# Leaving out some of the dummy matmuls among the last products and column sums of the first q

## The chip, the cores and the metric

The kernel runs on one core of a Trainium2 chip. The metric is the device time of one execution in microseconds (us). The profile counts from the start of the core's span, which is about 1.8 us shorter than the device time (809.5 and 811.27 us in the profiled execution of the kernel before).

PE is the matmul engine and PEld its weight load, which overlaps with PE (790.1 and 385.5 us busy in a span of 809.5 us). DVE and ACT are the vector and the scalar engine. POOL here issues the loads from memory, and SP issues transposes by DMA and stores.

## The reference, cut to what matters

```python
# q, k, v: (4, 6016, 256)
qn = q / (norm(q, axis=1) + 1e-6);  kn = k / (norm(k, axis=1) + 1e-6)
a  = softmax(kn.transpose(0, 2, 1) @ qn / tau)     # (4, 256, 256)
x  = (v @ a).reshape(24064, 256)
out = (silu(x @ w_gate) * (x @ w_val)) @ w_out     # d_ff = 1536
```

The kernel never makes x. For each batch it multiplies the 256 x 256 softmax into w_gate and w_val, in "units" of 128 x 512, and then runs v through the products (Wg and Wv). So the first batch has a start-up part that nothing hides: load k and q, form k-q products and norms, take the softmax, form the units. Then comes the dense stage, in which PE is busy to the end. The start-up of the other three batches runs in the background of the batch before.

## The kernel before: what the change and the argument touch

`keep_warm` is a matmul of ones that nobody reads. The loop over groups forms, for the last groups of q, the products and then the sums of squares column by column.

```python
    def keep_warm(n):
        ps = psum_o.tile([P, 2, C], FP32, tag="o")
        for _ in range(n):
            nc.tensor.matmul(ps, ones_bf, warm_bf, start=True, stop=True)
    # ... cut ...
    load_first_v()
    load_w(0, HW)                  # first half blocks of w_gate and w_val
    load_w(HW, WP)                 # second halves
    load_v(*allc[1])               # second chunk of v, then transposed by DMA
    transpose_v(*allc[1])
    for wc in range(1, NWC):
        load_w(wc * WP, (wc + 1) * WP)       # second and third blocks
    nc.gpsimd.dma_start(out=w_out_sb, ...)
    for g, which, gl in order:     # k groups, then q groups; NQ = 9, G_COLS = 5
        # ... cut: squares on ACT and DVE ...
        if which == 0:
            for t in ts:
                gemm1_pair(0, t)
            if g == G_COLS:
                first_cols(0)
            if g in (NQ - 4, NQ - 3):
                keep_warm(1)
        for t, sq in zip(ts, sqs):
            if which == 0 and g >= G_COLS:
                first_col_sums(0, t, sq)
            # ... cut ...
        if which == 0:
            # ... cut ...
            if G_COLS <= g < NQ - 2:
                keep_warm(NQ - 2 - g)
    first_softmax(0)               # holds three more dummies
```

The dense stage needs the second block of w_gate in its second step (f = 1), since each step forms two units ahead:

```python
        for f in range(FH):
            g_ps, v_ps, mv = gv_matmuls(b, ci, f)
            us = range(2 * f + 2, min(2 * f + 4, len(wp_units))) if gi == 0 else ()
            # ... cut: units us, silu, product, matmul with w_out of the chunk before ...
```

Each unit reads exT, the exponentials of the softmax, as weights. The other batches' norms come to DVE through memory: `norm_cols` writes a row out and reads it back broadcast to all partitions (ink), and `logits` multiplies with it on DVE fourteen steps later.

## Time and profile before

| | kernel before |
|---|---|
| device time, median of the first 3 runs | 812.73 us (812.66 to 813.35) |
| span of the profiled execution | 809.5 us |
| PE busy in the span | 790.1 us |
| PE busy from 40 us to 809 us | 762.4 us |
| last q load seen by DVE, softmax begins on ACT | 33.73 us, 35.04 us |
| second block of w_gate: landed, used by PE | 40.07 us, 40.20 us |

How to read it: from 40 us on PE has hardly a gap, so the last rows tell how early that part starts, and nothing before it counts unless it moves that start. Landing times are those of the loads' signals in the trace. The profile prints times to 0.01 us. The device time scatters (by 0.69 us in these three runs).

### The profile page before, as it was taken

What the parts mean: (1) busy time and instruction counts of PE and PEld (TensorE: products, weight loads), DVE (VectorE), ACT (ScalarE), POOL (GpSimd) and SP (SyncE); (2) the same over time, 40 slices, a digit from 0 to 9 for tenths busy, and PEclk for the clock granted to TensorE, in tenths of its full rate; (3) what the DMA queues carried; (4) which work ended last, traced back from release to release, by engine and by line L of the source; (5) the groups of instructions that cost most, each with busy time, mean ns of one, the idle gap of its engine ahead of it and who ended that gap; (6) DMA issues with size and microseconds to landing.
All of it is one profiled execution on the core that took longest, in us unless ns stands there. A gap on an engine that the chain in (4) does not pass through costs nothing.

```text
span 809.5 us, 11903 instructions
## 1 busy us (share of the span) xinstructions
PE 790.1 (98%) x3905; PEld 385.5 (48%) x3979; DVE 550.1 (68%) x841; ACT 455.6 (56%) x803; POOL 260.9 (32%) x320
## 2 busy tenths in 40 slices
PE   4999999999999999999999999999999999999998
PEld 2644444444454444444454444444445444444446
DVE  4777887658666778766766787866766665665654
ACT  4566666555555666555555666655555555555553
POOL 4415888431011787722010377742100000000000
PEclk9999999999999999999999999999999999999999
DMA  9995999659798899566889799763866656565533
GB/s 90 144 153 106 146 181 170 127 92 163 126 171 141 173 156 159 151 131 73 162 153 146 157 164 181 128 138 80 185 131 143 137 130 131 144 130 129 117 113 98
DMA packets 201070, 112.34 MB, mean 139 GB/s; under 512 B 149088, under 2 KB 187744, under 8 KB 200256
## 3 DMA queue, kind: packets, MB, share of 16 engines
q1 hardware_dynamic: 182720, 84.11, 44.0%
q0 software_dynamic: 18144, 27.41, 31.6%
q8 instruction: 31, 0.51, 0.3%
q14 instruction: 31, 0.25, 0.1%
q10 hardware_dynamic: 144, 0.07, 0.0%
HBM read 79.04 MB, written 60.43 MB: 172 GB/s over the span
## 4 chain that ended last, share of the span: by engine, by line
PE 95%; DMA 3%; issue 1%; ACT 0%; DVE 0%; POOL 0%; ACTq 0%; POOLq 0%
PE g_ps L439 30%; PE v_ps L439 30%; PE o_new L480 29%; PE ps L408 2%; DMA q_sb<-in_q_dram 2%; PE kq_new L168 2%; PE o_new L533 1%; DMA k_sb<-in_k_dram 1%; ACT silu L445 0%; PE last_ps L557 0%; DVE sv L449 0%; PE ss_new L195 0%; PE kq_new L173 0%; PE ps L398 0%; PE unit_ps L408 0%
## 5 line engine op out<-in xcount | busy, mean ns | idle before, releaser
L449 DVE TENSOR_TENSOR sv<-silu,v_ps 128x512 bf16<-128x512 bf16 (+1 forms) x576 | 387.3, 673 | 224.7 <-ACT silu L445 223.5
L445 ACT ACTIVATE silu<-g_ps 128x512 bf16<-128x512 f32 (+1 forms) x576 | 339.1, 589 | 292.9 <-PE g_ps L439 245.1
L439 PE MATMUL v_ps<-vT,Wv 128*128 128x512 bf16 (+1 forms) x1109 | 326.3, 374 | 1.2
L439 PE MATMUL g_ps<-vT,Wg 128*128 128x512 bf16 (+1 forms) x1105 | 325.8, 375 | 1.3
L480 PE MATMUL o_new<-sv,w_out_sb 128*128 128x512 bf16 (+1 forms) x1078 | 318.9, 375 | 1.2
L439 PEld LDWEIGHTS <-Wv 128*128 128x128 bf16 x1152 | 112.7, 98 | 131.0 <-issue 0.6
L300 POOL TENSOR_TENSOR acc_new<-acc_new,sq 128x512 f32<-128x512 f32 x135 | 156.1, 1156 | 56.0 <-DVE sq L290 41.9
L480 PEld LDWEIGHTS <-w_out_sb 128*128 128x128 bf16 x1104 | 108.0, 98 | 126.3
L439 PEld LDWEIGHTS <-Wg 128*128 128x128 bf16 x1152 | 109.6, 98 | 122.2
L126 POOL DMA_DIRECT2D vb_new<-in_v_dram x47 | 24.2, 516 | 265.5 <-DMA vT<-vb_new 264.6
L490 DVE COPY pl<-o_new 128x512 uint16<-128x512 uint16 (+1 forms) x92 | 62.3, 677 | 9.5 <-ACT pl L489 9.5
L290 DVE TENSOR_TENSOR sq<-q_sb 128x512 bf16<-128x512 fp8e5 x72 | 66.5, 924 | 0.0
L489 ACT COPY pl<-o_new 128x512 uint16<-128x512 uint16 (+1 forms) x92 | 53.2, 578 | 19.3 <-PE o_new L480 17.2
L291 ACT ACTIVATE sq<-k_sb 128x512 bf16<-128x512 fp8e5 x72 | 44.2, 615 | 0.0
L168 PE MATMUL kq_new<-k_sb,q_sb 128*128 128x512 fp8e5 x184 | 35.6, 319 | 0.9 <-DMA q_sb<-in_q_dram 0.9
L111 POOL DMA_DIRECT2D q_sb<-in_q_dram x45 | 25.2, 561 | 14.4 <-DMA k_sb<-in_k_dram 9.9
L168 PEld LDWEIGHTS <-q_sb 128*128 128x256 fp8e5 x184 | 22.9, 140 | 9.4 <-DMA q_sb<-in_q_dram 2.0
L195 PE MATMUL ss_new<-sq,ones_bf 128*128 128x256 bf16 x83 | 14.7, 334 | 11.1 <-ACT sq L185 11.1
L111 POOL DMA_DIRECT2D k_sb<-in_k_dram x42 | 22.9, 549 | 1.2 <-POOLq L741 0.8
L295 POOL TENSOR_TENSOR acc_new<-sq 128x512 f32<-128x512 bf16 x3 | 3.5, 1153 | 49.2 <-DVE sq L290 49.2
L195 PEld LDWEIGHTS <-ones_bf 128*128 128x128 bf16 x83 | 9.3, 117 | 15.1 <-issue 10.9
L408 PEld LDWEIGHTS <-exT 128*128 128x128 bf16 x104 | 10.0, 98 | 10.9 <-DMA w_gate_sb<-in_moe_w_gate_dram 0.2
(98 smaller groups left out, 209.0 us busy)
## 6 DMA issues: line engine op xcount, KB each, us to landing
rows<-pl SPq DMA_DIRECT2D x86, 256.0 KB, 3.1
out_dram<-ot_new SPq DMA_DIRECT2D x43, 512.0 KB, 4.0
vb_new<-in_v_dram POOLq DMA_DIRECT2D x43, 256.0 KB, 4.5
q_sb<-in_q_dram POOLq DMA_DIRECT2D x36, 128.0 KB, 6.4
k_sb<-in_k_dram POOLq DMA_DIRECT2D x33, 128.0 KB, 7.1
ot_new<-rows SPq DMA_TRANSPOSE x92, 3.7
k_sb<-in_k_dram POOLq DMA_DIRECT2D x5, 256.0 KB, 9.0
rows<-pl SPq DMA_DIRECT2D x6, 192.0 KB, 2.4
```

The source lines that it names most:

```text
L111: nc.gpsimd.dma_start(out=dst[:, gs:gs + gm, :], in_=src[b].rearrange("(p s) c -> p s c", s=NS)[:, gs:gs + gm, :])
L168: nc.tensor.matmul(kq[:, jh, :], q_sb[:, ps:ps + 2, js], k_sb[:, ps:ps + 2, :], start=(t == 0 and jh == 0), stop=last, perf_mode=DR, skip_ ...
L290: nc.vector.tensor_mul(sq[:, :pm, 0, :], q_sb[:, ps:ps + pm, :], q_sb[:, ps:ps + pm, :])
L291: nc.scalar.activation(sq[:, :pm, 1, :], k_sb[:, ps:ps + pm, :], ACT.Square)
L300: nc.gpsimd.tensor_tensor(out=acc, in0=acc, in1=sq[:, s, :, :], op=ALU.add)
L408: nc.tensor.matmul(ps, state[b, "exT"][:, jh, ih * P:(ih + 1) * P], (w_gate_sb, w_val_sb)[w][:, jh, cols], start=(jh == 0), stop=(jh == CH ...
L439: nc.tensor.matmul(dst[:, :mv], W[:, kk, fs], vT[:, kk, :mv], start=(kk == 0), stop=(kk == CH - 1))
L445: nc.scalar.activation(silu[:, :mv], g_ps[:, :mv], ACT.Silu)
L449: nc.vector.tensor_mul(sv[:, f, :mv], silu[:, :mv], v_ps[:, :mv])
L480: nc.tensor.matmul(self.o_ps[h][:, :self.mv], w_out_sb[:, f, h * P:(h + 1) * P], self.sv[:, f, :self.mv], start=(f == 0), stop=(f == FH - 1))
L489: nc.scalar.copy(pl[:, 0, :self.mv], halves[:, 0, :self.mv])
L490: nc.vector.tensor_copy(pl[:, 1, :self.mv], halves[:, 1, :self.mv])
```

## The change

The intent is to save PE time where dummies stand in front of real work. By its name, `keep_warm` is there for PE's clock; whether the clock needs these dummies was measured below (granted clock 1.00 from 26.40 to 40.05 us in q_none_sm, which has none).

```diff
-            if g in (NQ - 4, NQ - 3):
+            if g == NQ - 4:
                 keep_warm(1)
@@
-            if G_COLS <= g < NQ - 2:
-                keep_warm(NQ - 2 - g)
+            if g == G_COLS:
+                keep_warm(1)
```

With NQ = 9, group 5 had one dummy ahead of and two behind its sums, and group 6 one ahead and one behind. One ahead and one behind stay, in group 5.

## The prediction

> **What bounds the kernel now.** I read the page first, for which engine sets the span.
>
> ```profile
> span 809.5 us, 11903 instructions
> ...
> PE 790.1 (98%) x3905; PEld 385.5 (48%) x3979; DVE 550.1 (68%) x841; ACT 455.6 (56%) x803; POOL 260.9 (32%) x320
> ```
>
> PE (TensorE) is busy for 790.1 of 809.5 us, and from 40 us to the end the busy table by windows gives it 762.4 of 769.0 us. So there every microsecond by which PE starts that stage earlier, without meeting another wait, comes off the end. The change lies before it, in the last groups of the first q. There I read the chain of waits, in order of time.
>
> ```profile
> 32.88 0.46 PE ps L398 x2
> 33.34 0.44 PE kq_new L168 x4
> 33.77 0.23 PE ps L398
> 34.00 0.18 PE cols L218 x8
> 34.18 0.24 PE ps L398
> 34.42 0.22 PE kq_new L168 x2
> 34.64 0.23 PE kq_new L173 x2
> 34.87 0.14 PE cols L218 x6
> ...
> 35.04 0.18 ACT inq L224
> ```
>
> L398 is the dummy matmul, L168 and L173 the k-q products, L218 the column sums. The reader is to see that the dummies are not idle filling: between 32.88 and 35.01 each stands in PE's order ahead of real products or sums, and the softmax on ACT starts when the last sum is done. Then I asked whether PE would have had anything to do earlier, from the timelines of DVE and of PE with its weight loads.
>
> ```profile
> 33.73 0.42 DVE L182 TENSOR_TENSOR sq<-q_sb 128x256 bf16<-128x256 fp8e5 x1 [0.39 <-DMA q_sb<-in_q_dram]
> ```
> ```profile
> 39.76 0.59 PE L439 MATMUL v_ps<-vT_new,Wv 128*128 128x512 bf16 x2
> 40.20 1.03 PE L408 MATMUL ps<-w_gate_sb,exT 128*128 128x512 bf16 x4
> ```
> ```profile
> 40.11 0.61 PEld L408 LDWEIGHTS <-exT 128*128 128x128 bf16 x4 [0.25 <-DMA w_gate_sb<-in_moe_w_gate_dram]
> ```
>
> The columns are start, length, engine, line, operation; the bracket is the idle time before and what ended it. The square of the last q row waits for its load until 33.73 and ends at 34.15. At 40.11 the weight load for the second block of w_gate waits for a load from memory: it is released just in time for its matmul at 40.20, which follows the one before without a gap.
>
> [...] there is one cold window of 3.41 us, between two warm ones.
>
> ```profile
> 15.85:19.26 3.41, 1.59 (x12) 1.05 (x11) 1.90 (x3) 1.77 (x4) 0.97 (x2) 1.00 1.07 107
> 19.26:22.68 3.42, 3.29 (x15) 2.41 (x14) 1.72 (x4) 2.16 (x6) 0.62 (x2) 0.50 1.07 107
> 22.68:26.09 3.41, 2.98 (x27) 2.38 (x26) 2.21 (x6) 1.39 (x4) 0.53 (x1) 1.00 1.07 107
> 26.09:29.50 3.41, 2.97 (x26) 2.45 (x27) 2.75 (x5) 2.14 (x4) 1.44 (x2) 1.00 1.08 104
> ...
> 32.92:36.33 3.41, 3.41 (x39) 2.37 (x37) 2.08 (x7) 1.67 (x5) 3.09 (x5) 1.00 1.48 222
> ```
>
> After the length of each window come PE, weight loads, DVE, ACT and POOL busy, then the granted clock. A window with PE busy for 1.59 us (47%) was followed by a half clock; windows with 2.97 us (87%) were not. The window of the change has 3.41. [...] the two dummies behind the first sums start 215 ns apart, though each is shown 378 ns long, since the shown lengths overlap.
>
> **The change part by part.** The label speaks of four dummies of six. Comparing the instruction order of the two kernels, I count five in these groups before and two after, so three matmuls and their three weight loads go: the second of the pair behind the first group's sums, the one ahead of the second group's sums, and the one behind them. The other engines' orders are the same, no real matmul moves against another, and two allocations fewer in the two-deep rotation of that PSUM tag leave every later tile on the same buffer.
>
> Removed: 3 x 0.215 us = 0.65 us of PE time; the weight loads (96 ns each) lie beside matmuls and give nothing. All 0.65 us lie on the chain. What bounds them next: the last six sums start at 34.71 now and would start at 34.71 - 0.65 = 34.06; the last two of them read the square that ends at 34.15, plus some 0.05 us for the signal (the gap that the chain shows between engines is 0.02 to 0.05), so 34.20 where they start at 34.81 now. **That gives 0.6 us** at the start of the softmax: its first ACT instruction would move from 35.04 to about 34.4, the first product with exT from 36.66 to about 36.05.
>
> What the later stage meets when it comes 0.6 us early: the landings on the load queue, which PE does not steer. The loads are issued by POOL between 26 and 36 us, each released by an earlier landing, and the load engines are saturated there (share 1.0 to 1.5 in the windows). From the times of the landing signals in the trace, with the time of the first matmul that needs each: first v chunk 34.83 (needed 35.48), first half block of w_gate 35.48 (36.66), of w_val 36.16 (36.87), second half of w_gate 36.88 (37.60), of w_val 37.55 (38.90), **second block of w_gate 40.07 (40.20)**, of w_val 41.33 (42.04), third of w_gate 42.59 (43.77). Those up to 38.90 have at least 0.65 us of slack, so the 0.6 us just passes them. The second block of w_gate has 0.13 us, of which the signal and the weight load (0.04 + 0.10) use all. So PE would be ready at 40.20 - 0.6 = 39.6 and wait until 40.20: -0.65 from the dummies, +0.05 for the square, +0.6 in the new wait. **Sum: about 0.** From 40.20 on PE would be where it was, and the rest of the span is the same program. If the landing moves a little against PE from one execution to the next, some 0.1 us of the 0.6 may survive, so I expect 812.73 - 0.1 = 812.6 us.
>
> **Rivals.** First, the whole 0.6 us survives (812.1 us): that needs the second w_gate block to land 0.6 us earlier in relation to PE in the timed executions. For it: I see one execution only, and that one took 811.27 us where the timed ones took 812.66 to 813.35. Against it: q and w_gate share one saturated queue, so they shift together. Second, the clock falls: [...] PE runs up to 3.4 us at half clock. If that hits the dense stage from 36 us on, it loses at most 1.7 us, of which up to 0.6 us was to be waited for w_gate anyway, so +1.1 to +1.7 us, about 814.1 us. For it: the clock did fall in this kernel at 47% busy[...]. Against it: after the change no PE gap between 31 and 40 us is estimated above 0.6 us, and the window of the change keeps roughly 3.41 - 0.65 = 2.8 us busy or more (81%), since real work moves up into it[...]. [...] this keeps a chance of some 8%. Third, transfers hide everything already before the change, the q loads being the bound: I put 0.05 us of the 0.65 down to that; it would be more if the last q row landed later than 33.7, and the outcome is again zero.
>
> **Range and chances.** The centre is 812.6. Downwards the full 0.65 us plus the spread of the kernel before (0.7 us from lowest to highest) gives 811.6; upwards half a cold window or the same spread gives 813.6. Two per cent would be 16.3 us, 25 times the PE time removed and nearly ten times the worst cold window, so either side gets one per cent.
>
> **What would show it right or wrong.** In the changed profile: (1) L398 on PE three fewer (records of single matmuls can be missing, so count its weight loads: 8 before, 5 after); (2) the first ACT instruction on the column sums some 0.6 us earlier in relation to the last q square; (3) a PE wait of about 0.6 us on the load of w_gate just ahead of the second block's matmuls near 40.2 us, where there was none; (4) granted clock 1.00 from 23 us on; (5) from there the same PE busy time to the end. I would be wrong if the clock shows 0.50 in any window after 30 us, if no wait on w_gate appears and the end is 0.6 us earlier, or if the time moves by over 1.5 us, which nothing here can explain.

0.65 us off for three dummies (215 ns between the starts of two of them), 0.05 us back for the square and 0.6 us back for the new wait come to about 0, and the 0.1 us that may survive gives 812.6 us. A "warm" window is a stretch with the granted clock at 1.00, a "cold" one a stretch with 0.50. The 1.7 us of the second rival are an estimate from the one record of 3.41 us at 0.50: in it matmuls of 256 columns start 213 to 214 ns apart, in the record of 1.00 before it mostly 108 to 109 ns. In q_before_v, run later, two such stretches at 0.50 follow each other. The 8% is the author's estimate; in the one trace there was then, nothing between 47 and 87% busy had been seen at a recorded clock.

## The result, and the profile after

| | before | after |
|---|---|---|
| device time, median of 4 runs | 813.04 us (812.66 to 813.95) | 813.19 us (811.37 to 813.47) |
| ratio after / before | | 0.9995 (0.9978 to 1.0013) |
| span of the profiled execution | 809.5 us | 811.6 us |

The interval in brackets behind a ratio is the 95% one. Ratios are the mean time of one kernel's fast runs over that of the other's of the same rounds, so not quite the ratio of the medians quoted. The lines below answer to those that the prediction shows of before. First PE's timeline of the changed kernel (start, length, engine, line, operation, count, and in brackets the idle time before with what ended it):

```profile
32.61 0.38 PE L398 MATMUL ps<-warm_bf,ones_bf 128*128 128x512 bf16 x1
32.75 0.67 PE L168 MATMUL kq_new<-k_sb,q_sb 128*128 128x512 fp8e5 x4
33.50 0.35 PE L218 MATMUL cols<-ones_bf,sq 128*128 128x1 bf16 x8
...
34.19 0.38 PE L218 MATMUL cols<-ones_bf,sq 128*128 128x1 bf16 x6
...
39.28 0.59 PE L439 MATMUL v_ps<-vT_new,Wv 128*128 128x512 bf16 x2
40.28 1.04 PE L408 MATMUL ps<-w_gate_sb,exT 128*128 128x512 bf16 x4 [0.41 <-DMA w_gate_sb<-in_moe_w_gate_dram]
```

Only one dummy is left behind the first sums, products follow sums directly, and PE is done with its second step about half a microsecond earlier (39.28 instead of 39.76). Then it stands still. The bracket's 0.41 us counts from the modelled end of the matmul before; by starts, the next matmul would have followed at 39.71 (two matmuls, 0.216 us each) and came at 40.28, which is 0.57 us lost. The weight load ahead of it shows the same wait from its own side:

```profile
40.27 0.55 PEld L408 LDWEIGHTS <-exT 128*128 128x128 bf16 x4 [0.90 <-DMA w_gate_sb<-in_moe_w_gate_dram]
```

The chain of waits, asked for the stretch from 31 to 43 us, no longer runs over dummies, sums and softmax. It runs over the load:

```profile
33.65 6.58 DMA w_gate_sb<-in_moe_w_gate_dram
40.23 0.04 issue
40.28 1.04 PE ps L408 x4
```

The softmax itself did start earlier. ACT's first instruction on the column sums, before and then after:

```profile
35.04 0.17 ACT L224 ACTIVATE inq<-cols 128x2 f32<-128x2 f32 x1 [1.10 <-PE cols L218]
```

```profile
34.61 0.17 ACT L224 ACTIVATE inq<-cols 128x2 f32<-128x2 f32 x1 [0.51 <-PE cols L218]
```

In this execution the last q square began at 33.89 instead of 33.73, because its load landed later. Measured from that square, ACT starts 0.72 us after it instead of 1.31 us: 0.59 us earlier.

One step further the two traces differ once more. PE at the second block of w_val, before and then after:

```profile
42.04 1.02 PE L408 MATMUL ps<-w_val_sb,exT 128*128 128x512 bf16 x4
```

```profile
42.02 1.03 PE L408 MATMUL ps<-w_val_sb,exT 128*128 128x512 bf16 x4
```

By the spacing of the starts this matmul comes 0.12 us late in the kernel before (its weight load stands behind 0.24 us of "issue", for which the profile shows no wait) and in time in the changed one. What makes that gap is not shown.

**Where the 2.1 us between the two profiled spans come from.** Step by step the changed kernel is 0.09 us behind at 40.28 us and 0.02 us ahead from 42 us on, and then it falls behind near 184 and near 378 us. The timeline of DVE near 184 us, of before and then of the changed kernel:

```profile
181.71 0.48 DVE L344 SCALAR_TENSOR_TENSOR s_new<-kq_new,inv,ink 128x256 f32<-128x256 f32 x1
```

```profile
183.51 0.48 DVE L344 SCALAR_TENSOR_TENSOR s_new<-kq_new,inv,ink 128x256 f32<-128x256 f32 x1 [1.73 <-DMA ink<-row]
```

DVE waits 1.73 us for the broadcast norms (ink) of the next batch, holds up the products behind it, and PE then waits for DVE (idle for 0.33 us before its matmul at 184.64 us and for 0.90 us before that at 379.69 us). The dummies stand far from this, and the kernel before has timed runs as long (up to 813.95 us), so I take it for a wait that comes in some executions and not in others. So the first experiment made the ground quiet.

### The profile page after: what moved, and what is told of

Same layout as the page of the kernel before. It is cut to its first block, busy times and chain, and to the rows that moved or that the text cites. A ratio compares the mean times of both kernels' runs of the same rounds, so it can differ in the third digit from the quotient of the medians.

```text
span 811.6 us, 11971 instructions
## 1 busy us (share of the span) xinstructions
PE 794.5 (98%) x3976; PEld 385.4 (47%) x3976; DVE 550.2 (68%) x841; ACT 455.3 (56%) x803; POOL 260.6 (32%) x320
## 4 chain that ended last, share of the span: by engine, by line
PE 89%; DMA 9%; POOL 1%; DVE 1%; issue 1%; ACT 0%; DVEq 0%; POOLq 0%
PE g_ps L439 28%; PE v_ps L439 28%; PE o_new L480 27%; DMA row<-inv 3%; PE ps L408 2%; DMA q_sb<-in_q_dram 2%; PE kq_new L168 2%; DMA k_sb<-in_k_dram 2%; DMA ink<-row 1%; PE o_new L533 1%; DMA w_gate_sb<-in_moe_w_gate_dram 1%; DVE sv L449 1%; POOL k_sb L111 0%; POOL inv L330 0%; POOL inv L328 0%
## 5 line engine op out<-in xcount | busy, mean ns | idle before, releaser
L439 PE MATMUL v_ps<-vT,Wv 128*128 128x512 bf16 (+1 forms) x1128 | 330.5, 375 | 1.5 <-DVE sv L449 1.2
L439 PE MATMUL g_ps<-vT,Wg 128*128 128x512 bf16 (+1 forms) x1128 | 330.9, 375 | 0.0
L480 PE MATMUL o_new<-sv,w_out_sb 128*128 128x512 bf16 (+1 forms) x1104 | 324.7, 376 | 0.0
```

The lines of the kernel that those rows point to most:

```text
L439: nc.tensor.matmul(dst[:, :mv], W[:, kk, fs], vT[:, kk, :mv], start=(kk == 0), stop=(kk == CH - 1))
L480: nc.tensor.matmul(self.o_ps[h][:, :self.mv], w_out_sb[:, f, h * P:(h + 1) * P], self.sv[:, f, :self.mv], start=(f == 0), stop=(f == FH - 1))
```

## The experiments

The theory: the three dummies cost PE their full time on the chain, and their removal gives it back, but the second block of w_gate lands when it lands, so PE waits there instead. Rival 1: the dummies only filled time in which PE waited for q anyway. Rival 2: the clock falls without them and eats a gain. Rival 3: there is a plain gain, and the scatter hides it.

**Quiet ground, and the second chunk of v moved: four kernels on one chip.** In all four, `logits` and all that follows it in the background of a batch come three steps later, so that ink has landed:

```diff
-    plan[S1 + 24].append((logits, 0))
+    plan[S1 + 27].append((logits, 0))
     ... and so on with each later step of that plan, + 3
```

The kernels are q_before (the kernel before, so changed), q_after (with the three dummies left out) and the two with a suffix v, in which the load that precedes the suspected one is moved behind it (in this diff and in those below, arguments and repeated lines are put in words):

```diff
     load_w(HW, WP)
+    load_w(WP, 2 * WP, w_gate only)
     load_v(*allc[1])
     transpose_v(*allc[1])
-    for wc in range(1, NWC):
+    load_w(WP, 2 * WP, w_val only)
+    for wc in range(2, NWC):
         load_w(wc * WP, (wc + 1) * WP)
```

> The kernel before, with one thing changed in the other batches only: logits and what follows them come three steps later, so that they find the broadcast of the norms landed. The changed kernel's profile shows about 0.5 and 1.3 us lost there (near 184 and 378 us), the profile of before nothing, and the timed runs lie in two groups near 811.4 and 813.2 us. If that wait is the scatter: about 811.3 us in nearly all runs, ratio to before near 0.998. If not: 813.0 us and the same scatter. It is to be the quiet ground for the three runs beside it.

> The same quiet ground with the three dummies left out. Theory (the time saved goes into a wait for the second block of w_gate): softmax about 0.5 us earlier, PE waits about 0.6 us near 40.2 us for that load, end within 0.1 us of q_before. Rival 1 (the dummies filled time in which PE waited for q anyway): softmax not earlier, no new wait, end the same. Rival 2 (clock): granted clock 0.50 in a window after 30 us, 1 us or more slower. Rival 3 (a plain gain hidden by scatter): 0.6 us faster than q_before.

> q_before with the load of the second v chunk moved behind the second block of w_gate, which should land about 1.2 us earlier. Theory: with the dummies in place PE has no wait there to lose, so within 0.1 us of q_before. Rival (that load held up PE before too): about 0.6 us or more faster.

> q_after with the same move of the v load. Theory: the wait near 40.2 us is gone and the 0.5 to 0.6 us reach the end: 0.5 us faster than q_after, q_before and q_before_v, perhaps 0.05 less because the second block of w_val comes just in time. Rival 1: no difference to q_before_v. Rival 3: no more than q_after already gained.

| 5 timed runs each | median | lowest to highest | mean | PE starts the second w_gate block |
|---|---|---|---|---|
| q_before | 811.01 us | 810.91 to 811.91 | 811.18 | 40.20 us, no wait |
| q_after | 811.40 us | 810.68 to 812.06 | 811.31 | 39.91 us, after a wait |
| q_before_v | 810.98 us | 810.88 to 811.99 | 811.20 | 40.07 us, no wait |
| q_after_v | 810.79 us | 810.40 to 811.10 | 810.75 | 39.64 us, no wait |

The kernel before took 810.99 to 813.50 us in the same rounds. The four never exceed 812.06, and no profile of a kernel with the later logits shows DVE waiting for ink, which fits the ink wait as the upper part of the scatter, though no single ratio to before leaves the noise. One run in five near 811.9 remained; what that is shows below.

The theory's pattern is there. Rival 1 falls: the softmax begins 0.75 us after the last square in q_after (34.19 us) and 1.27 us in q_before (34.98 us). Rival 2 falls in the executions profiled: the granted clock is 1.00 from 24 us on in all four. Rival 3, 0.6 us of plain gain, does not show in the means (811.18 and 811.31 us). PE's timeline of q_after and q_after_v at the second block:

```profile
38.82 0.59 PE L439 MATMUL v_ps<-vT_new,Wv 128*128 128x512 bf16 x2
39.91 1.04 PE L408 MATMUL ps<-w_gate_sb,exT 128*128 128x512 bf16 x4 [0.49 <-DMA w_gate_sb<-in_moe_w_gate_dram]
```

```profile
39.21 0.59 PE L439 MATMUL v_ps<-vT_new,Wv 128*128 128x512 bf16 x2
39.64 1.03 PE L408 MATMUL ps<-w_gate_sb,exT 128*128 128x512 bf16 x4
```

The order of two loads alone makes the wait appear or vanish. With the dummies in place the same move changes nothing in the mean (811.18 and 811.20). Without them it takes 0.56 us off the mean (811.31 to 810.75), where 0.5 was expected. With five runs each the times support this and do not prove it; the positions in the profiles do. In the profiled execution of q_after w_gate landed at 39.86, 0.21 us earlier than in q_before, and its span is the shortest of the four (808.9 us). From 42 us to the end PE is 0.40 us ahead of q_before there, so some 0.19 us of the lead are left even when the earlier landing is taken off.

The profiled execution of q_after_v also shows the next wall. PE at the first use of the moved v chunk:

```profile
52.42 0.61 PE L439 MATMUL g_ps<-vT,Wg 128*128 128x512 bf16 x2 [0.40 <-DMA vT<-vb_new]
```

The chunk's transpose landed at 52.38 (49.28 in before), and there this execution lost again all that it had gained.

**Three dummies more, the load one transfer later, no dummies at all, and a repair: four kernels on a second chip.**

> q_before with three more dummies in the same places (two behind the first group's sums, one behind the second's). Theory: each dummy is 0.216 us on the chain to the softmax and PE reaches the second block of w_gate without slack, so the softmax and everything from there on is 0.65 us later than in q_before and the end too: 811.65 us. Rival 1 (dummies fill time in which PE waits for q): no shift. The same step that is worth nothing downwards should cost its full size upwards.

```diff
-                keep_warm(NQ - 2 - g)
+                keep_warm(4 if g == G_COLS else 2)
```

PE's timeline of q_before, then of q_before_p3:

```profile
32.26 0.39 PE L398 MATMUL ps<-warm_bf,ones_bf 128*128 128x512 bf16 x1
...
34.65 0.29 PE L218 MATMUL cols<-ones_bf,sq 128*128 128x1 bf16 x6
```

```profile
33.47 0.39 PE L398 MATMUL ps<-warm_bf,ones_bf 128*128 128x512 bf16 x1
...
36.52 0.29 PE L218 MATMUL cols<-ones_bf,sq 128*128 128x1 bf16 x6
```

From the first dummy to the last sums q_before_p3 takes 3.05 us; q_before needs 2.39 us. That is 0.66 us more for three dummies, against 0.65 expected, so in this stretch each dummy costs its full 0.22 us. (The 0.216 us of the expectation stand between the starts of the last two dummies in the trace of the kernel before.) The median is 812.27 us; the repeat of q_before on the same chip, told below, has 811.11. That is 1.16 us more where 0.65 was expected. The three fastest runs (811.47, 811.47, 811.75) are 0.4 to 0.7 us above the usual 811.0 to 811.1. The other three took 812.80 to 813.12 us; the one of them that was profiled (813.08 us) had a late q load, for which PE waited 1.17 us. So the positions show the 0.65 us; the timed runs fit it only if the slow three are set aside after the fact.

> q_after with w_val loaded ahead of w_gate in the second block, so that the load under suspicion lands one transfer (1.2 to 1.3 us) later. Theory: the PE wait near 40.2 us grows by 1.2 to 1.3 us and so does the time, to about 812.6 us. Rival 1 and rival 3 (that wait is not what bounds the start of the dense stage): no change.

```diff
-        load_w(WP, 2 * WP)                     # w_gate, then w_val
+        load_w(WP, 2 * WP, w_val, then w_gate)
```

PE's timeline:

```profile
41.26 1.04 PE L408 MATMUL ps<-w_gate_sb,exT 128*128 128x512 bf16 x4 [1.69 <-DMA w_gate_sb<-in_moe_w_gate_dram]
```

The wait grew from 0.49 to 1.69 us, by 1.20 us as expected. The median is 812.36 us. q_after was not on this chip in these rounds, so the pair was run again (below).

> q_after without any dummy at all: the two left in the groups and the three of the softmax are gone too. Theory: no further gain, since the last square of q and then the w_gate load bound PE; the wait near 40 us is about the same or some 0.1 us longer, the time within 0.2 us of q_after, if the clock holds. If the clock falls without dummies (rival 2): granted clock 0.50 in a window between 33 and 40 us, the dense stage 1 us or more later, 812.4 us or more.

```diff
             if g == NQ - 4:
-                keep_warm(1)
...          (all calls of keep_warm, also the two in first_softmax)
```

The busy times of this kernel in stretches of 3.41 us, the length of the clock record at 0.50 in the kernel before (length; PE, weight loads, DVE, ACT, POOL busy; then granted clock, DMA share, GB/s):

```profile
29.81:33.22 3.41, 3.26 (x33) 2.61 (x30) 2.87 (x6) 1.69 (x3) 1.75 (x3) 1.00 1.17 131
33.22:36.64 3.42, 2.81 (x38) 2.11 (x38) 2.43 (x9) 2.02 (x6) 3.08 (x6) 1.00 1.58 243
```

The clock held with PE busy for 2.81 of 3.42 us (82%). PE waits for w_gate by 0.42 us and starts the block at 40.16. The median of 4 runs is 810.95 us (810.61 to 812.12). None of the eight dummies was needed for the clock in this execution, and without the last five the time stayed within the scatter.

> q_after_v, whose gain of 0.4 us was lost again at 52 us because the moved v chunk was transposed late beside the load of w_out: here the second half of w_out is loaded two steps into the dense stage instead. Theory: the transposed chunk lands before 51.8 us, no PE wait at 52 us, and the end is 0.4 to 0.5 us earlier than q_before and 0.3 to 0.5 us earlier than q_after_v, near 810.5 us. If the chunk is late for another reason than w_out, PE waits there as in q_after_v.

```diff
-    nc.gpsimd.dma_start(out=w_out_sb, ...)            # all 256 columns
+    load_w_out(0)                                     # 128 columns
...  (in the dense loop)
+            if now == 2:
+                load_w_out(1)
```

Its profile did what was expected: no wait at 52 us, the moved chunk's matmuls at 51.87 instead of 52.40 in q_before, the span 808.7 us. The timed runs did not follow. They lie between 810.53 and 814.28 us, three of six above 812, median 811.73. Something that the one profile does not show goes wrong in other executions; I did not pursue it, so this stays open. It is no improvement.

**The pair again with its control, and a candidate: four kernels on the second chip.** The first three are the same files as before.

> q_before again, as the control on the chip of the three runs beside it: PE reaches the second block of w_gate near 40.2 us without a wait, about 811.0 us where no load of q straggles.

> q_after again beside its two variants. Theory: within 0.3 us of q_before_2, with a PE wait of 0.4 to 0.6 us on w_gate. A plain gain of the change would show as 0.6 us less.

> w_val ahead of w_gate again, now beside q_after on one chip: by the theory 1.2 to 1.3 us longer than q_after_2 in the same rounds, since the first run showed the wait at 1.69 us where q_after had 0.49; if the wait does not set the end, the same time.

> No dummies at all, and the load of the second v chunk behind the second block of w_gate: the candidate that may beat both kernels. Theory: the clock holds as in q_none_sm, no wait near 40 us, PE about 0.5 us ahead of q_before there; at 52 us PE waits for the transposed v chunk as in q_after_v and loses up to that gain again. So between 810.4 and 811.0 us, at best 0.5 us under q_before_2, and under the kernel before by that and by the norm wait that the later logits avoid.

| runs on the second chip | median | lowest to highest |
|---|---|---|
| kernel before, 12 runs | 812.11 us | 811.23 to 814.51 |
| q_before_2, 6 runs | 811.11 us | 810.92 to 811.91 |
| q_after_2, 4 runs | 811.26 us | 811.02 to 811.52 |
| q_after_vf_2, 4 runs | 812.38 us | 811.95 to 812.40 |
| q_none_sm_v, 6 runs | 810.87 us | 810.50 to 811.40 |

q_after_vf_2 is 1.12 us above q_after_2 by medians and their ranges do not touch. Expected were 1.2 to 1.3; by the profiles PE starts the block at 41.17 instead of 40.25, 0.92 us later. So a shift of that load's landing goes to the end nearly in full. q_before and q_after are equal again: over both chips the mean is 811.25 us for 11 runs with all dummies and 811.29 us for 9 runs without the three.

The control showed something that the prediction had not allowed for. PE in its profiled execution (811.83 us):

```profile
40.97 1.03 PE L408 MATMUL ps<-w_gate_sb,exT 128*128 128x512 bf16 x4
```

PE is 0.77 us late here without any wait for w_gate, which landed at 40.05 as ever. One of the sixteen parts of a q load landed at 32.07, more than a microsecond after the other fifteen (30.71); PE's longest wait for a q load is 1.0 us in this profile and 0.5 us in that of q_before. Two more of the 11 runs of q_before lie near 811.9; they were not profiled, and I take them for the same. The profiled execution of q_after_vf_2 had the same straggler (31.95), and there it cost nothing, since the wait absorbed it:

```profile
39.80 0.59 PE L439 MATMUL v_ps<-vT_new,Wv 128*128 128x512 bf16 x2
41.17 1.04 PE L408 MATMUL ps<-w_gate_sb,exT 128*128 128x512 bf16 x4 [0.78 <-DMA w_gate_sb<-in_moe_w_gate_dram]
```

The wait shrank from 1.69 to 0.78 us, the block began at 41.17 instead of 41.26, and the two executions took 811.95 and 812.03 us. So without the dummies PE has slack in front of the load, and a late q eats into the slack first. The same late load stands in four of the fourteen profiles (also in q_before_p3 and q_none_sm_v), each time 1.2 to 1.5 us behind its other parts.

q_none_sm_v is faster than the kernel before, with a ratio of 0.9983 and an interval of 0.9970 to 0.9995. Most of it comes from the later logits: q_before_2 alone has 0.9986 (0.9973 to 1.0000). It counts as "same" by the 2% bar, and it was not run beside the changed kernel as given. I take it as the best version found. Its profiled execution, the slowest of the six (811.40 us), did not show the expected lead: with a q load late at 32.28 us PE started the block at 40.17, where q_before has 40.20, and it waits 0.19 us for the transposed chunk at 52 us.

## Why the prediction was right, point by point

The measured 813.19 us lies in the range of 811.6 to 813.6 us around 812.6, and "within 2%" was right. A range of 2 us tests little about an effect of 0.6 us, so the steps count more. The lower edge does not follow from its own terms, either: 812.73 less 0.65 and 0.7 is 811.4, and one timed run of the changed kernel took 811.37 us.

1. *Three matmuls go.* Right: the weight loads of the dummy are 8 before and 5 after.
2. *Each dummy stands on the chain with 0.215 us, and the last q square leaves 0.6 us of the 0.65.* Right: 0.59 us earlier measured from that square. Upwards three dummies cost 0.66 us.
3. *The first halves of the weight blocks just let the 0.6 us pass.* Nearly right. The nearest was the first half of w_val, which landed at 36.32 and was used at 36.37, about 0.07 us late by the spacing of the starts.
4. *The second block of w_gate takes it all back.* The mechanism is right: 0.57 us lost by starts where 0.6 was written, in a place where before had no wait. Moving that landing earlier or later moved PE with it. "All" is some 0.2 us too much. The 0.13 us between landing and use were not all needed for the signal and the weight load: in the changed kernel the matmul follows the landing by 0.05 us (40.23 to 40.28).
5. *The clock holds.* Right in every profile taken here, from 24 us on to the last microsecond or so. That PE's busy time from 40 us on stays the same cannot be read off: 762.4 us before and 766.6 us after, but with 3706 and 3776 matmuls on record; the weight loads agree (3776, 365.7 us). The prediction gave the fall 8%, by the author's estimate; with no dummy at all the clock held too (1.00 at 82% busy in q_none_sm).
6. *The q loads and w_gate shift together because they share a queue* (the argument against the first rival). It holds between the first two profiles (the last q load and w_gate each 0.16 us later), but not always: a single late part of one q load moves PE by 0.77 us and leaves w_gate where it was. In such an execution the dummies' removal does save: with the late part at 31.95 us (q_after_vf_2) PE is 0.73 us earlier at the end of its second step than with it at 32.07 us (q_before_2), so by my estimate some 0.6 us are due to the three dummies, and w_gate in its usual place (40.05 us) would have left nearly all of it. How much this gives on average is not shown.
7. *Some 0.1 us may survive.* The times do not resolve it: 813.04 and 813.19 us, and 811.25 and 811.29 us; the difference of the latter two has a 95% interval (my estimate from the single runs) of 0.35 us faster to 0.43 us slower, which leaves out a gain of 0.6 us and not one of 0.2. The profiles do: w_gate landed 0.16 us later in the changed kernel's execution and PE is 0.02 us ahead from 42 us on, and q_after, q_after_2 and q_none_sm against q_before give the same. Reckoned from the landing, 0.18 to 0.19 us survive: 0.08 us of point 4, the rest the gap at 42 us.
8. *A move of over 1.5 us could not be explained.* Single executions do move by 2 us. This was taken for spread without a cause; much of it is the wait of DVE for the broadcast norms in the other batches (1.73 us near 184 us and 2.30 us near 378 us in the changed kernel's profile, none in the profiles with later logits).

## What to carry to other kernels

Before you count a saving on the chain, list the landing times of what the next stage needs beside the times at which it is used. Here a use that followed its landing by 0.13 us had hardly any slack (0.08 us could be used; in the changed kernel the matmul still came 0.05 us after the landing), though the profile showed no idle time of PE at all. Here that co-limit was visible only as 0.25 us of waiting of an engine that overlaps with the bound one (PEld). Taking 0.65 us away ahead of it left some 0.2 us; adding 0.65 us moved the chain by all of it. And where the effect is smaller than the scatter, find what scatters first and judge by positions in the profile.

## What the traces show of the clock and of the parts of a load

- In the kernel before, the trace records a granted clock of 1.00 from 15.85 to 19.26 us, of 0.50 from 19.26 to 22.68 us and of 1.00 from there to the end of the span. In the 3.41 us ahead of the fall PE was 47% busy, and its longest gaps were those in these lines of PE's timeline.

```profile
17.20 1.12 PE L195 MATMUL ss_new<-sq,ones_bf 128*128 128x256 bf16 x8 [0.88 <-ACT sq L185]
19.32 1.65 PE L195 MATMUL ss_new<-sq,ones_bf 128*128 128x256 bf16 x7 [1.00 <-ACT sq L185]
```

- PE's busy time is as the profile shows it, with modelled ends of the matmuls. In eleven of the fourteen profiles the mean granted clock is 0.995 to 0.998, and in the 3.41 us ahead of the first record at 0.50 PE was busy for 1.39 to 1.71 us (41 to 50%). In the other three (q_after, q_best and q_none_sm_v) the mean is 1.0; the lowest stretch read there, in q_after, had 1.81 us (53%), with a gap of 1.02 us in it, and the next 3.41 us are at 1.00 too. Nothing between these was seen, and whether the busy share is what decides is not shown. The last groups had 82% without any dummy in q_none_sm (71% in one stretch of q_none_sm_v), at 1.00. In q_before_v a stretch at 0.50 with 2.58 us busy (76%, 14.48 to 17.89 us) was followed by another at 0.50.

```profile
16.25:19.66 3.41, 1.81 (x14) 1.19 (x13) 2.32 (x4) 2.29 (x4) 1.05 (x2) 1.00 1.07 107
```

- The granted clock reads 1.00 before its first record, at 15.85 us in the kernel before, though eight matmuls of 256 columns took 1.87 us at 9.80 and 1.05 us at 22.75, after the record at 0.50. So the reading before the first record does not fit the matmuls.
- Each transfer leaves sixteen landing signals in the trace, here called its parts (6912 for 432 transfers in the kernel before), and PE went on after the last one: in the changed kernel 15 parts of the second block of w_gate were in by 39.64 us and the last at 40.23, and the weight load that waited for them began at 40.27. Of the second half of w_gate 15 parts were in by 36.29 us and the last at 37.05. In the fourteen profiles the last part of the loads that landed from 32 to 38 us was 0.36 to 0.85 us behind the fifteenth (0.38 to 0.48 in the kernel before, 0.67 to 0.77 in the changed one), and 1.2 to 1.5 us for one q load in four of them. The trace does not tell what makes that part late.
